# First four steps of the first block on unsplit float32 operands, in a fused attention and two-MoE kernel

## The chip, the cores and the metric

The kernel runs on one core of a Trainium2 chip. The metric is the device time of one execution in microseconds (us); lower is better. Before the change the median of three runs is 680.03 us (679.96 to 680.19). A difference of 0.2% is 1.36 us.

The engines are named as the profile names them: PE (matrix multiply) with PEld (its weight loads), DVE, ACT and POOL (elementwise work), SP (which only issues DMA loads and stores here; SPq in the trace). Each engine works through its own instructions in program order.

## The reference, cut to what matters

```python
x = window_attention(q, k, v)              # 4 x 8 heads x 576 tokens x 64, window 64
x = x.transpose(0, 2, 1, 3).reshape(2304, 512)
# first MoE layer, a plain feed-forward of 2048 hidden units:
h = x @ w_in                               # 512 -> 2048
g = where(h >= 1, h, where(h <= -1, 0, (h + 1) ** 2 / 4))
x = g @ w_out                              # 2048 -> 512
# second: 8 experts of 1024 hidden units, each token goes to one
e = argmax(x @ w_gate, axis=1)
out = gate[:, None] * (relu(x @ w1[e]) @ w2[e])
```

`w_in` and `w_out` come as 64-bit floats, everything else as 32-bit floats.

## The kernel before

**Tokens and blocks.** The 2304 tokens are 18 chunks of 128. A chunk has two attention units of four heads each (unit u = 2 x chunk + half), so there are 36 units. The first feed-forward works on five blocks of 384, 512, 512, 512 and 384 tokens (`BLOCKS`); the first block needs units 0 to 5.

**A unit** is a chain over all engines: `qk` on PE (scores, four products of 32-bit floats for each of two head pairs, line 393, after four mask products in bfloat16, line 389), `mx` on DVE (row maximum), `nm`, four exponentials `exa` to `exd` on ACT (line 427), `rb`, `rc` and `nrm` (division by the row sum, line 444, DVE or POOL), `tr` on PE (four transposes, line 471), `pb` (copy out, line 475 or 477), `av` on PE (eight products of 32-bit floats, line 486). Its result, 128 tokens by 256 values, is split into two parts that PE takes in its fast float format: `hi` (ACT, line 508) is the value rounded to that format and `lo` (DVE, line 510) is what is left.

**A feed-forward step** is one slice of 128 hidden units for one block. PE makes `h` from three passes, `w_hi x_hi`, `w_lo x_hi`, `w_hi x_lo`, of four products each (`ga`, line 603: 12 products of 384 columns in the first block). ACT and DVE make the activation (`rl`, `sq`, `st`, lines 614 to 619) and split it into `gh` and `gl` (lines 625, 627). Then `gb` (line 653) multiplies it with the same slice of `w_out`, again three passes, for three chunks: nine products of 512 columns. `acc` stays in PSUM over the sixteen steps of a block.

**A weight slice** is loaded (`lw`, 512 KB, line 292), turned from a 64-bit into a 32-bit float by one ACT and three DVE instructions (`ab`, `sa`, `sb`, `s`, lines 310 to 320) and split into two parts (`hc` on ACT, line 324; `wl` on DVE or POOL, line 326). The slices come in the order in-0, in-1, out-0, in-2, out-1, in-3, and so on; `lw`, `ab`, ... carry that place as number.

**What sets the order.** The list `HEAD` names every part of the work; each name runs one generator to its next `yield`. The order of the names is the order of the instructions on PE, DVE, ACT and POOL (`in_order`) and on SP. Tuples such as `WLO_P` or `PB_V` choose an engine for single instructions. In the first stage `lu` loads the queries and keys of a unit (320 KB, line 348), `lv` its values (256 KB, line 359). DMAs use eight semaphores in turn, so the load that is n-th on SP waits for the landing of the (n-8)-th.

PE starts with 17 products on zeros (line 1121) and a few more between the first units (`wm`, line 1241, and `KEEP_T`, line 468), which fill time in which there is no data yet. The program's later parts, which the change reaches only through the order of `HEAD` and the tuples, are the routing to experts, the second layer (lines 603 and 653 too) and the rows left over (lines 1052 to 1100).

Of the kernel before, what the change touches and what calls it, by code (L numbers as in the profile page):

```python
# [9 lines left out]
F32 = mybir.dt.float32  # L10
F32R = mybir.dt.float32r
BF16 = mybir.dt.bfloat16
I32 = mybir.dt.int32
U32 = mybir.dt.uint32
U16 = mybir.dt.uint16
ACTF = mybir.ActivationFunctionType
# [18 lines left out]
PJ_V = (3, 4, 6, 8, 11, 12, 13, 14, 19, 21, 23, 24, 26, 27, 28, 30, 35)  # L35
PS_V = ((15, 0), (17, 1))
# [4 lines left out]
ELO_P = (1, 2, 3, 7, 9, 10, 14)  # L41
LLO_P = (5, 7, 10, 13, 14)
YO_V = ((0, 3), (1, 1), (1, 2), (1, 3), (3, 0), (3, 1), (3, 2))
# [132 lines left out]
PB_V = (0, 2, 3, 6, 7, 14, 15, 16, 18, 19, 20, 23, 25, 29, 30, 31, 33, 35)  # L176
PL_V = ((15, 0), (15, 1), (31, 0), (31, 1), (47, 2), (47, 3), (63, 0), (63, 1), (63, 2), (63, 3))
PP_A = (14, 15, 16, 18, 20, 24, 25, 27, 29, 32, 33, 34)
KEEP_T = {0: 1, 1: 4}
KEEP_Q = {}  # L180
NM_P = (1, 2, 3, 7)
RB_P = (2, 5, 6, 7, 8)
# [1203 lines left out]
```

## Time and profile before

| | |
|---|---|
| median of the runs | 680.03 us |
| profiled execution | 679.67 us |
| its span, first to last instruction | 677.9 us |
| PE busy | 666.9 us (98%) |
| DVE, ACT, POOL busy | 416.1, 391.7, 105.4 us |
| granted TensorE clock, mean over the span | 0.997 |

The span is 1.77 us shorter than the profiled execution, and that is 0.36 us under the median. The chain that ended last lies on PE for 90% of the span, 43% of it in `gb` (line 653) and 42% in `ga` (line 603). In the page's slices a digit is the busy share in tenths of a slice of 16.9 us. PE is below 9 in the first and the last slice only. A matmul's record overlaps its neighbours' (they are pipelined), so what a product costs is read from the distance of starts, not from its duration.

### The profile page before, as it was taken

Reading aid. Unit: us, or ns where it says so; the run is one execution under the profiler, and the core shown is the slowest. Engines: PE = TensorE matmul, PEld = TensorE weight load, DVE = VectorE, ACT = ScalarE, POOL = GpSimd, SP = SyncE. Lnnn points to the kernel's source line nnn. Section 1 sums busy time; section 2 is a strip of 40 time slices with the busy share of each in tenths; the row PEclk is TensorE's granted clock in tenths of the full one; section 3 lists DMA queues with packets and bytes.
Section 4 is the critical chain, followed back from the end, with each engine's and each line's share of the span. In section 5 each row is a group of like instructions: output and inputs, shape, how many; then the busy total and the mean of one; then the engine's idle time right before and its main releaser. Section 6 shows DMA issues by size and latency. Waiting matters only on the chain.

```text
span 677.9 us, 11422 instructions
## 1 busy us (share of the span) xinstructions
PE 666.9 (98%) x4187; PEld 556.4 (82%) x4187; DVE 416.1 (61%) x858; ACT 391.7 (58%) x969; POOL 105.4 (16%) x93
## 2 busy tenths in 40 slices
PE   8899999999999999999999999999999999999996
PEld 4788998888888888888888889988888888888885
DVE  6999997435453414535233355889987799665541
ACT  6998887465636546545455344777666466443340
POOL 2542212300220102013101002230010000001110
PEclk9999999999999999999999999999999999999998
DMA  9993642135431313252122225344532232213342
GB/s 343 397 406 126 228 133 56 32 86 141 131 118 39 113 35 83 69 161 66 64 48 78 47 109 195 102 138 117 141 94 84 66 93 62 62 62 94 112 137 74
DMA packets 77500, 80.43 MB, mean 119 GB/s; under 512 B 46231, under 2 KB 51607, under 8 KB 77314
## 3 DMA queue, kind: packets, MB, share of 16 engines
q1 hardware_dynamic: 77138, 79.12, 37.6%
q8 instruction: 33, 0.54, 0.3%
q0 software_dynamic: 160, 0.43, 0.2%
q14 instruction: 25, 0.20, 0.1%
q10 hardware_dynamic: 144, 0.13, 0.1%
HBM read 54.32 MB, written 14.94 MB: 102 GB/s over the span
## 4 chain that ended last, share of the span: by engine, by line
PE 90%; ACT 3%; DMA 2%; DVE 1%; issue 1%; POOLq 0%; DVEq 0%; ACTq 0%; SPq 0%
PE acc L653 43%; PE h L603 42%; PE av L486 2%; PE S L393 2%; ACT sr L427 1%; DMA out_dram<-y 1%; DMA out_dram<-yl,idx 0%; DMA R<-out_dram 0%; DMA er<-in_w_dram 0%; ACT t L310 0%; PE pt L471 0%; ACT wl L842 0%; DVE wl L844 0%; DVE mx L547 0%; ACT wi L324 0%
## 5 line engine op out<-in xcount | busy, mean ns | idle before, releaser
L603 PE MATMUL h<-xT,wi 128*128 128x512 f32 (+1 forms) x960 | 208.3, 369 | 0.5 <-DVE pb L475 0.3
L603 PEld LDWEIGHTS h<-xT,wi 128*128 128x128 f32 x960 | 175.0, 188 | 25.6 <-DVE pb L475 0.6
L653 PE MATMUL acc<-wo,ghi 128*128 128x512 f32 x576 | 145.7, 393 | 0.0
L653 PEld LDWEIGHTS acc<-wo,ghi 128*128 128x128 f32 x576 | 106.9, 188 | 22.2 <-issue 0.7
L619 DVE SCALAR_TENSOR_TENSOR a<-h,a 128x512 f32<-128x512 f32 (+1 forms) x80 | 50.4, 633 | 107.9 <-ACT a L616 106.7
L614 ACT ACTIVATE a<-h,half 128x512 f32<-128x512 f32 (+1 forms) x80 | 51.6, 646 | 91.8 <-PE h L603 83.5
L603 PE MATMUL h<-xT,we 128*128 128x512 f32 (+1 forms) x480 | 103.1, 369 | 0.0
L603 PEld LDWEIGHTS h<-xT,we 128*128 128x128 f32 x480 | 84.1, 188 | 15.1
L627 POOL TENSOR_TENSOR glo<-a,ghi 128x512 fp32r<-128x512 f32 (+1 forms) x38 | 48.0, 1265 | 242.8 <-ACT ghi L625 202.2
L653 PE MATMUL acc<-wo,glo 128*128 128x512 f32 x288 | 78.4, 389 | 0.0
L653 PE MATMUL acc<-we,ghi 128*128 128x512 f32 x290 | 72.6, 389 | 0.0
L653 PEld LDWEIGHTS acc<-wo,glo 128*128 128x128 f32 x288 | 54.1, 188 | 11.5
L653 PEld LDWEIGHTS acc<-we,ghi 128*128 128x128 f32 x290 | 53.9, 188 | 10.8
L745 DVE CUSTOM_DVE_ANT_0 junk<-xg,wgb 128x512 bf16<-128x512 f32 x76 | 58.2, 766 | 2.7 <-DMA xg<-x2s 2.0
L625 ACT ACTIVATE ghi<-a 128x512 fp32r<-128x512 f32 (+1 forms) x80 | 46.5, 585 | 18.9 <-DVE a L619 11.1
L761 ACT ACTIVATE gpr<-gpr 128x512 f32<-128x512 f32 x68 | 39.8, 586 | 24.2 <-DVE gpr L753 23.5
L753 DVE TENSOR_TENSOR gpr<-xg,wgb 128x1024 f32<-128x1024 f32 x34 | 41.8, 1229 | 12.1 <-ACT gpr L761 10.4
L616 ACT ACTIVATE a<-a 128x512 f32<-128x512 f32 (+1 forms) x80 | 46.9, 588 | 1.3
L635 ACT ACTIVATE ghi<-h 128x512 fp32r<-128x512 f32 (+1 forms) x40 | 22.0, 551 | 44.0 <-PE h L603 31.1
L627 DVE TENSOR_TENSOR glo<-a,ghi 128x512 fp32r<-128x512 f32 (+1 forms) x42 | 27.7, 661 | 32.0 <-ACT ghi L625 27.7
L653 PE MATMUL acc<-we,glo 128*128 128x512 f32 (+1 forms) x145 | 39.5, 388 | 0.0
L637 DVE SCALAR_TENSOR_TENSOR glo<-h,ghi 128x512 fp32r<-128x512 f32 (+1 forms) x40 | 25.2, 633 | 20.3 <-ACT ghi L635 20.0
(176 smaller groups left out, 742.0 us busy)
## 6 DMA issues: line engine op xcount, KB each, us to landing
qk<-in_qq_dram SPq DMA_DIRECT2D x26, 320.0 KB, 4.0
er<-in_w_dram SPq DMA_DIRECT2D x32, 256.0 KB, 3.1
wraw<-in_wi_dram SPq DMA_DIRECT2D x14, 512.0 KB, 8.6
wraw<-in_wo_dram SPq DMA_DIRECT2D x14, 512.0 KB, 7.5
vt<-in_vv_dram SPq DMA_DIRECT2D x26, 256.0 KB, 3.4
xg<-x2s SPq DMA_DIRECT2D x18, 256.0 KB, 2.8
out_dram<-y SPq DMA_DIRECT2D x17, 256.0 KB, 2.3
x2s<-xrow SPq DMA_DIRECT2D x8, 512.0 KB, 3.8
```

Of the source, the lines that this page charges most:

```text
L603: nc.tensor.matmul(h[:, :n], w[:, wa, k * P:k * P + P], x[:, xa, k, o:o + n], start=(i == 0), stop=(i == 3 * KD - 1),)
L614: nc.scalar.activation(a[:, :n], h[:, :n], ACTF.Relu, scale=0.5, bias=half[:, 0:1])
L616: nc.scalar.activation(a[:, :n], a[:, :n], ACTF.Square)
L619: nc.vector.scalar_tensor_tensor(out=a[:, :n], in0=h[:, :n], scalar=1.0, in1=a[:, :n], op0=ALU.max, op1=ALU.min)
L625: nc.scalar.activation(hi[:, :n], a[:, :n], ACTF.Copy)
L627: (nc.gpsimd if pool else nc.vector).tensor_tensor(out=lo[:, :n], in0=a[:, :n], in1=hi[:, :n].bitcast(F32), op=ALU.subtract)
L635: nc.scalar.activation(hi[:, :n], h[:, :n], ACTF.Relu)
L637: nc.vector.scalar_tensor_tensor(out=lo[:, :n], in0=h[:, :n], scalar=0.0, in1=hi[:, :n].bitcast(F32), op0=ALU.max, op1=ALU.subtract,)
L653: nc.tensor.matmul(a[:, cols], ga[:, t * P:t * P + P], w[:, wa, cols], start=(first and j == 0), stop=(last and j == 2 and (not by_tile or ...
L745: nc.vector.tensor_tensor_reduce(out=junk, in0=xg[t], in1=Z["wgb"][:, e], scale=1.0, scalar=0.0, op0=ALU.mult, op1=ALU.add, accum_out=Z["L ...
L753: nc.vector.tensor_tensor(out=pr, in0=xg[t].unsqueeze(1).to_broadcast([P, 2, DM]), in1=Z["wgb"][:, e:e + 2], op=ALU.mult,)
L761: nc.scalar.activation(pr, pr, ACTF.Copy, accum_out=Z["L"][:, t, e:e + 1])
```

## The change

For the first four steps of the first block (`NF = 4`) PE multiplies the 32-bit floats themselves: one product where there were three. A weight slice of these steps can be used as soon as its 32-bit float is made (after `s`); its two parts are made later, since the other blocks use them. A unit's result in the first block is first copied whole (`xw`, a new ACT instruction), and `hi` and `lo` are made from that copy, `lo` on POOL for three of the six units (`XLO_P`). The activation of these steps isn't split: `gh` and `gl` are gone for steps 0 to 3. On PE `ga` is four products of 384 columns in these steps instead of 12, and `gb` three of 512 instead of nine. All of `HEAD` and most engine tuples are new ("order searched"); of these the diff shows a line or two.

```diff
-PB_V = (0, 2, 3, 6, 7, 14, 15, 16, 18, 19, 20, 23, 25, 29, 30, 31, 33, 35)
-KEEP_T = {0: 1, 1: 4}
+PB_V = (0, 1, 2, 3, 4, 5, 15, 17, 18, 20, 21, 24, 25, 26, 30, 31, 33)
+KEEP_T = {0: 2, 1: 5}
+NF = 4
+XLO_P = (0, 4, 5)
...
@@ -282,6 +285,7 @@
         return a.rearrange("p (a k) -> p a k", k=P)
 
     win, wout = {}, {}
+    whole_i, whole_o, whole_x = {}, {}, {}
 
     def load_w(kind, f):
         src = wi if kind == "i" else wo
@@ -305,8 +309,11 @@
 
     def split_parts(kind, f, raw):
         hw, lw = raw[:, :, 1], raw[:, :, 0]
-        t = att.tile([P, 512], I32, tag="t", name="t", bufs=TB1)
-        w = wp.tile([P, 2, 512], F32R, tag="w", name="w" + kind)
+        if f < NF:
+            t = wp.tile([P, 512], I32, tag="w", name="tw")
+        else:
+            t = att.tile([P, 512], I32, tag="t", name="t", bufs=TB1)
+            w = wp.tile([P, 2, 512], F32R, tag="w", name="w" + kind)
         nc.scalar.activation(t.bitcast(F32), hw.bitcast(F32), ACTF.Abs, scale=2.0**-112)
         yield
         nc.vector.tensor_scalar(
@@ -320,7 +327,11 @@
         nc.vector.scalar_tensor_tensor(
             out=t, in0=hw, scalar=-0x80000000, in1=t, op0=ALU.bitwise_and, op1=ALU.bitwise_or
         )
-        yield
+        if f < NF:
+            (whole_i if kind == "i" else whole_o)[f] = t.bitcast(F32)
+        yield
+        if f < NF:
+            w = wp.tile([P, 2, 512], F32R, tag="w", name="w" + kind)
         nc.scalar.activation(w[:, 0], t.bitcast(F32), ACTF.Copy)
         yield
         (nc.gpsimd if wseq_at[kind, f] in WLO_P else nc.vector).tensor_tensor(
@@ -501,10 +512,24 @@
         av = heads(bank("h" if alt else "acc", "av"))
         av_mm(s, av)
         yield
+        o = P * c - blocks[b][0]
+        if b == 0:
+            if hf not in whole_x:
+                whole_x[hf] = wp.tile([P, 2, BLOCKS[0]], F32, tag="w", name="xw")
+            xw = whole_x[hf][:, :, o:o + P]
+            nc.scalar.activation(xw, av[:, :2], ACTF.Copy)
+            del av
+            yield
         x_tile(b)
-        o = P * c - blocks[b][0]
         hi = xT[b][:, 0, 2 * hf:2 * hf + 2, o:o + P]
         lo = xT[b][:, 1, 2 * hf:2 * hf + 2, o:o + P]
+        if b == 0:
+            nc.scalar.activation(hi, xw, ACTF.Copy)
+            yield
+            (nc.gpsimd if u in XLO_P else nc.vector).tensor_tensor(
+                out=lo, in0=xw, in1=hi.bitcast(F32), op=ALU.subtract
+            )
+            return
         nc.scalar.activation(hi, av[:, :2], ACTF.Copy)
         yield
         nc.vector.tensor_tensor(out=lo, in0=av[:, :2], in1=hi.bitcast(F32), op=ALU.subtract)
@@ -606,6 +631,25 @@
                 )
                 i += 1
         return h
+
+    def whole_parts(w, n):
+
+        h = ps.tile([P, 512], F32, tag="h", name="h", bufs=2)
+        for k in range(KD):
+            nc.tensor.matmul(
+                h[:, :n], w[:, k * P:k * P + P], whole_x[k // 2][:, k % 2],
+                start=(k == 0), stop=(k == KD - 1),
+            )
+        yield
+        a = gp.tile([P, NG], F32, tag="ghi", name="aw")
+        nc.scalar.activation(a[:, :n], h[:, :n], ACTF.Relu, scale=0.5, bias=half[:, 0:1])
+        yield
+        nc.scalar.activation(a[:, :n], a[:, :n], ACTF.Square)
+        yield
+        nc.vector.scalar_tensor_tensor(
+            out=a[:, :n], in0=h[:, :n], scalar=1.0, in1=a[:, :n], op0=ALU.max, op1=ALU.min
+        )
+        return a
 
     def act_parts(x, w, o, n, pool):
         h = layer1(x, w, o, n)
@@ -1200,6 +1244,22 @@
     def step_parts(i):
         ph, b, f, t0, t1 = steps[i]
         if ph == 1:
+            if b == 0 and f < NF:
+                a = yield from whole_parts(whole_i.pop(f), blocks[0][1])
+                yield
+                for t in of_tiles(i):
+                    if began[t] == i:
+                        acc[t] = bank("acc", "acc")
+                for t in of_tiles(i):
+                    nc.tensor.matmul(
+                        acc[t], a[:, t[2] * P:t[2] * P + P], whole_o[f],
+                        start=began[t] == i, stop=ended[t] == i,
+                    )
+                del a, whole_o[f]
+                if f == NF - 1:
+                    whole_x.clear()
+                yield
+                return
             g[i] = yield from act_parts(xT[b], win[f], t0 * P, (t1 - t0) * P, i in GLO_P)
             if i == max(ended[1, b, t] for t in range(blocks[b][1] // P)):
                 del xT[b]
@@ -1251,7 +1311,7 @@
     KIND = {}
     for names, fn in (
         ("ab sa sb s hc wl", lambda k: split_parts(*pend.pop(0))),
-        ("qk mx nm exa exb exc exd rb rc nrm pp tr pb av hi lo", lambda k: (late_parts if k >= 2 * PAIR else unit_parts)(k)),
+        ("qk mx nm exa exb exc exd rb rc nrm pp tr pb av xw hi lo", lambda k: (late_parts if k >= 2 * PAIR else unit_parts)(k)),
         ("qkp mkp mxp nmp rbp rcp avp hip lop", both_parts),
         ("ga rl sq st gh gl rh rv gb", step_parts),
         ("lw", once(lambda k: pend.append(load_w(*wseq[k])))),
```

**PE, from the first step's `ga` on.** `pt` are transposes, `av` the product with the values, `h<-xT,wi` and `acc<-wo` the split steps. Before:

```order
L389 MATMUL Sa<-cb 64x128
L393 MATMUL Sa<-qqr 64x128 x4
L603 MATMUL h<-xT,wi 128x384 x12
L471 MATMUL pt<-ct,sr 128x128 x4
L603 MATMUL h<-xT,wi 128x384 x12
...
L393 MATMUL S<-qk 64x128 x4
L603 MATMUL h<-xT,wi 128x384 x12
L486 MATMUL av<-pb,vte 64x64 x8
L471 MATMUL pt<-ct,sr 128x128 x8
L603 MATMUL h<-xT,wi 128x384 x12
L486 MATMUL av<-pb,vte 64x64 x8
L653 MATMUL acc<-wo,ghi 128x512 x6
```

In the changed kernel (`h<-xw,tw` and `acc<-tw,aw` are the unsplit steps; two `ga` in a row read as x8):

```order
L404 MATMUL Sa<-qqr 64x128 x4
L639 MATMUL h<-xw,tw 128x384 x8
L482 MATMUL pt<-ct,sr 128x128 x4
L400 LDWEIGHTS cb
...
L404 MATMUL S<-qk 64x128 x4
L639 MATMUL h<-xw,tw 128x384 x4
L482 MATMUL pt<-ct,sr 128x128 x4
L497 MATMUL av<-pb,vte 64x64 x8
L482 MATMUL pt<-ct,sr 128x128 x4
L639 MATMUL h<-xw,tw 128x384 x4
L1254 MATMUL acc<-tw,aw 128x512 x3
L497 MATMUL av<-pb,vte 64x64 x16
```

The work between the first `ga` and the fourth `gb` is the same set; the first two `ga` now stand together, ahead of the transposes of unit 6, and the unit products are spread in another way.

**SP, the 22nd to 33rd load of the kernel before and the 21st to 28th of the changed one** (`qqr` and `qk` are queries and keys, `vte` and `vt` values, `wraw` weights; in brackets the semaphores that the load waits for). Before, `vte` with DMAHW6 is the values of unit 5, and `qqr` with DMAHW0 the queries of unit 9:

```order
L348 DMA qqr<-in_qq_dram 128x640 [waits DMAHW5_49]
L359 DMA vte<-in_vv_dram 128x512 [waits DMAHW6_49]
L359 DMA vte<-in_vv_dram 128x512 [waits DMAHW7_49]
L348 DMA qqr<-in_qq_dram 128x640 [waits DMAHW0_49]
L292 DMA wraw<-in_wo_dram 128x1024 [waits DMAHW1_49]
L348 DMA qk<-in_qq_dram 128x640 [waits DMAHW2_49]
L359 DMA vt<-in_vv_dram 128x512 [waits DMAHW3_49]
L359 DMA vte<-in_vv_dram 128x512 [waits DMAHW4_49]
L348 DMA qk<-in_qq_dram 128x640 [waits DMAHW5_49]
L292 DMA wraw<-in_wi_dram 128x1024 [waits DMAHW6_49]
L348 DMA qk<-in_qq_dram 128x640 [waits DMAHW7_49]
L292 DMA wraw<-in_wo_dram 128x1024 [waits DMAHW0_49,DVE_49,Activation_49]
```

Now the values of unit 5 are `vte` with DMAHW6, the queries of unit 9 the `qqr` behind it:

```order
L370 DMA vte<-in_vv_dram 128x512 [waits DMAHW4_49]
L359 DMA qqr<-in_qq_dram 128x640 [waits DMAHW5_49]
L370 DMA vte<-in_vv_dram 128x512 [waits DMAHW6_49]
L359 DMA qqr<-in_qq_dram 128x640 [waits DMAHW7_49]
L296 DMA wraw<-in_wo_dram 128x1024 [waits DMAHW0_49]
L296 DMA wraw<-in_wi_dram 128x1024 [waits DMAHW1_49]
L296 DMA wraw<-in_wo_dram 128x1024 [waits DMAHW2_49,PE_49]
L359 DMA qk<-in_qq_dram 128x640 [waits DMAHW3_49]
```

The values of unit 5 are the 23rd load in both, behind the same 22 loads in another order: `lw0` to `lw5`, `lu0` to `lu8`, `lv0` to `lv4`, the masks and the constants. The queries of unit 9 were the 25th load and are the 24th.

**ACT, shortly before the first `ga`.** Before, `xT` is `hi`, `wi` a weight's first part, `pb` the copy of a transposed unit:

```order
L508 ACTIVATE xT<-av 128x2x128
L427 ACTIVATE sr,sm<-S,nm 128x128 x2
L477 ACTIVATE pb<-pt 128x512
L310 ACTIVATE t<-wraw 128x512
L427 ACTIVATE sr,sm<-S,nm 128x128 x2
L508 ACTIVATE xT<-av 128x2x128
L477 ACTIVATE pb<-pt 128x512
L324 ACTIVATE wi<-t 128x512
L508 ACTIVATE xT<-av 128x2x128
L427 ACTIVATE sr,sm<-Sa,nm 128x128
L508 ACTIVATE xT<-av 128x2x128
L419 ACTIVATE nm<-mx 128x4
```

Now (`xw` is the whole copy, `xT<-xw` is `hi`, `tw` a weight slice on its way to a 32-bit float):

```order
L527 ACTIVATE xT<-xw 128x2x128
L438 ACTIVATE sr,sm<-S,nm 128x128 x2
L317 ACTIVATE tw<-wraw 128x512
L520 ACTIVATE xw<-av 128x2x128
L438 ACTIVATE sr,sm<-Sa,nm 128x128
L520 ACTIVATE xw<-av 128x2x128
L527 ACTIVATE xT<-xw 128x2x128
L520 ACTIVATE xw<-av 128x2x128
L438 ACTIVATE sr,sm<-Sa,nm 128x128
L527 ACTIVATE xT<-xw 128x2x128
L317 ACTIVATE tw<-wraw 128x512
L438 ACTIVATE sr,sm<-S,nm 128x128
```

The first parts of weights and the copies `pb` are gone from this stretch, and `hi` of a unit no longer stands ahead of the first `ga`: `xw` does.

## Rows read from the trace of the kernel before

**Rows 1.** The page: busy time of PE, and the slices of PE and DMA
```profile
PE 666.9 (98%) x4187; PEld 556.4 (82%) x4187; DVE 416.1 (61%) x858; ACT 391.7 (58%) x969; POOL 105.4 (16%) x93
...
PE   8899999999999999999999999999999999999996
...
DMA  9993642135431313252122225344532232213342
```

**Rows 2.** Stretches: us, each engine's busy us (count), PE clock, DMA share, GB/s
```profile
10.00:20.00 10.00, 8.80 (x177) 5.98 (x174) 9.16 (x26) 9.82 (x48) 6.76 (x9) 1.00 1.04 400
20.00:30.00 10.00, 8.53 (x159) 6.85 (x158) 9.66 (x24) 9.98 (x40) 5.01 (x8) 1.00 1.04 395
40.00:50.00 10.00, 10.00 (x78) 8.59 (x77) 10.00 (x23) 9.51 (x27) 2.05 (x2) 1.00 1.03 408
200.00:300.00 100.00, 100.00 (x630) 82.18 (x629) 36.92 (x55) 55.31 (x131) 12.04 (x9) 1.00 0.34 91
```

**Rows 3.** Timeline of PE, 26 to 62 us: start, length, instructions, idle before
```profile
27.26 2.37 PE L603 MATMUL h<-xT,wi 128*128 128x384 f32 x12
29.93 0.63 PE L471 MATMUL pt<-ct,sr 128*128 128x128 f32 x4 [0.29 <-DVE sr L444]
...
38.27 2.38 PE L603 MATMUL h<-xT,wi 128*128 128x384 f32 x12 [0.35 <-DVE pb L475]
...
51.57 0.66 PE L471 MATMUL pt<-ct,sr 128*128 128x128 f32 x4
51.98 1.64 PE L653 MATMUL acc<-wo,ghi 128*128 128x512 f32 x6
...
54.14 1.52 PE L653 MATMUL acc<-wo,ghi 128*128 128x512 f32 x6
55.50 0.84 PE L653 MATMUL acc<-wo,glo 128*128 128x512 f32 x3
56.18 2.27 PE L603 MATMUL h<-xT,wi 128*128 128x384 f32 x12
58.28 0.60 PE L471 MATMUL pt<-ct,sr 128*128 128x128 f32 x4
```

**Rows 4.** Timeline of PE, 64.1 to 64.4 us: products of 32-bit floats
```profile
64.05 0.25 PE L389 MATMUL S<-cb 64*64 64x128 bf16 x4
64.12 0.39 PE L393 MATMUL S<-qk 64*64 64x128 f32 x8
64.35 0.23 PE L389 MATMUL S<-cb 64*64 64x128 bf16 x4
```

**Rows 5.** Timeline of SP (issues), 24 to 27 us
```profile
24.16 0.33 SPq L348 DMA_DIRECT2D qk<-in_qq_dram  x1
24.84 0.33 SPq L292 DMA_DIRECT2D wraw<-in_wi_dram  x1
25.51 0.33 SPq L348 DMA_DIRECT2D qk<-in_qq_dram  x1
26.41 0.33 SPq L292 DMA_DIRECT2D wraw<-in_wo_dram  x1
```

**Rows 6.** DMA issues, 0 to 30 us: count, KB each, median us to landing
```profile
qqr<-in_qq_dram SPq DMA_DIRECT2D x10, 320.0 KB, 7.0
...
vte<-in_vv_dram SPq DMA_DIRECT2D x9, 256.0 KB, 7.0
```

**Rows 7.** Waits of PE, 0 to 60 us: total us, times, longest
```profile
PE av L486 <- DMA vte<-in_vv_dram: 0.5, 1, 0.5
```

**Rows 8.** Chain of waits, 20 to 30 us: start, us, what
```profile
25.22 0.49 ACT pb L477
25.71 0.52 ACT wi L324
26.23 0.27 ACT xT L508
```

More of the change, by code (lines that the diff above doesn't have):

```diff
@@ L34 @@
 EARLY = 10
-PJ_V = (3, 4, 6, 8, 11, 12, 13, 14, 19, 21, 23, 24, 26, 27, 28, 30, 35)
-PS_V = ((15, 0), (17, 1))
+PJ_V = (1, 2, 4, 5, 6, 8, 9, 15, 17, 19, 21, 24, 25, 26, 27, 30, 31, 34)
+PS_V = ((15, 0), (15, 1), (16, 1), (17, 0), (17, 1))
 DT0 = 14
@@ L40 @@
 PBB = 2
-ELO_P = (1, 2, 3, 7, 9, 10, 14)
-LLO_P = (5, 7, 10, 13, 14)
-YO_V = ((0, 3), (1, 1), (1, 2), (1, 3), (3, 0), (3, 1), (3, 2))
+ELO_P = (0, 5, 8, 10, 13, 15)
+LLO_P = (2, 3, 4, 7, 8, 9, 12, 13, 14, 15)
+YO_V = ((2, 0), (3, 2), (3, 3))
 SCRATCH = 4096
@@ L58 @@
 HEAD = (
[112 rows of a table removed]
-).split()
-NRM_P = (0, 1, 2, 3, 4, 5, 8, 9, 10, 14, 15, 16, 17, 20, 21, 28, 30, 31, 33, 34)
-WLO_P = (2, 3, 4, 6, 20, 22, 27, 28)
-GLO_P = (0, 3, 4, 5, 6, 9, 15, 18, 19, 20, 21, 24, 26, 27, 29, 30, 31, 34, 36, 37, 39, 40, 41, 46, 48, 50, 51, 52, 54, 56, 59, 67, 68, 69, 70, 72, 73, 77)
-PB_V = (0, 2, 3, 6, 7, 14, 15, 16, 18, 19, 20, 23, 25, 29, 30, 31, 33, 35)
-PL_V = ((15, 0), (15, 1), (31, 0), (31, 1), (47, 2), (47, 3), (63, 0), (63, 1), (63, 2), (63, 3))
-PP_A = (14, 15, 16, 18, 20, 24, 25, 27, 29, 32, 33, 34)
-KEEP_T = {0: 1, 1: 4}
[113 rows of a table added]
+).split()
+NRM_P = (0, 1, 2, 3, 4, 5, 7, 8, 9, 12, 15, 16, 17, 19, 27, 28, 30, 33, 34, 35)
+WLO_P = (1, 3, 6, 13, 16, 20, 26, 28, 30)
+GLO_P = (13, 18, 19, 21, 23, 25, 34, 35, 37, 39, 41, 43, 45, 49, 51, 54, 56, 57, 59, 62, 64, 65, 66, 67, 69, 70, 72, 79)
+PB_V = (0, 1, 2, 3, 4, 5, 15, 17, 18, 20, 21, 24, 25, 26, 30, 31, 33)
+PL_V = ((15, 0), (15, 1), (15, 2), (31, 3), (63, 0), (63, 2), (63, 3))
+PP_A = (15, 16, 24, 25, 30, 32, 35)
+KEEP_T = {0: 2, 1: 5}
 KEEP_Q = {}
-NM_P = (1, 2, 3, 7)
-RB_P = (2, 5, 6, 7, 8)
+NM_P = (0, 1, 6, 7, 8)
+RB_P = (3, 4, 6, 7, 8)
+NF = 4
+XLO_P = (0, 4, 5)
 WARM = 17
```

225 rows, old and new, of the table HEAD are left out of this document.

## The prediction

> **What bounds the kernel now.** I read the page first: PE is busy for 98% of the span, and its slices are full except the first and the last [rows 1]. So the time is PE's work, plus what PE loses at both ends. The table of stretches then says where it loses: from 10 to 30 us PE is busy for 8.5 to 8.8 of every 10 us, from 40 us on for all of it [rows 2]. In the first 30 us two other things are full as well: ACT, with 9.82 and 9.98 of 10 us, and the DMA engines, with a share of 1.04 at 395 to 400 GB/s [rows 2]. At 200 to 300 us ACT is at 55 of 100 and DMA at 0.34, with PE at 100 [rows 2]. What the change does is thus worth what it does to one moment: the one from which PE never waits again. PE's timeline shows it. The first `ga` starts at 27.26, behind it there are two waits that the profile names, 0.29 and 0.35 us, and from 38.27 on there is none [rows 3]. I take the start of the seventh `ga`, 56.18 us [rows 3], as the mark: the same work stands before it in both kernels, and behind it PE runs full. What moves the mark moves the end.
>
> **What the change takes from PE and adds to it.** In an undisturbed place a split `ga` (12 products of 384 columns) takes 2.10 us, from 56.18 to 58.28, and a split `gb` (nine of 512) 2.04 us, from 54.14 to 56.18 [rows 3]. The fifth step and all later ones stay split.
>
> No row shows a product of 32-bit floats over the whole array, so its price is bounded by the nearest rows. The scores are such products, on quarters of the array. The order lists four of them where the trace counts eight instructions: a product is two instructions. Eight of 128 columns take from 64.12 to 64.35, and as four quarters work side by side that is two in a row, 0.115 us each, 0.90 ns per column [rows 4]. A transpose is one such instruction over the whole array: four of 128 columns from 51.57 to 51.98 are 0.80 ns per column [rows 3]. So an unsplit `ga` is 4 x 2 x 384 columns, 2.46 to 2.76 us, and an unsplit `gb` is 3 x 2 x 512 columns, also 2.46 to 2.76 us. Against 2.10 and 2.04 a step grows by 0.36 + 0.42 = 0.78 to 0.66 + 0.72 = 1.38 us, four steps by 3.1 to 5.5 us. I take the middle, 4.3, since a dense product has the scores' form and the transposes' place in the array. All of it is on PE, the bound, and nothing hides it; only an earlier start can pay for it.
>
> A rule of the Trainium skill bears on this (FP8 and Floating Point Precision, TensorE Precision Notes): a true FP32 product takes four passes through the array. By that, with a pass at the price that a pass has here (2.10 / 12 = 0.175 us for 384 columns, 2.04 / 9 = 0.227 for 512 [rows 3]), `ga` would be 16 passes, 2.80 us, and `gb` 12 passes, 2.72 us; four steps would grow by 5.5 us. The rows' own rate gives 3.1 to 5.5, so the rule stands at the dear end.
>
> **What the earlier start gives back.** Before the first `ga`, ACT no longer makes first parts of weights (0.52 us each) nor copies of transposed units (0.49), and the whole copy takes the place of `hi` (0.27) [rows 8]; DVE loses the second parts and the `lo`. If those queues alone decided, the first `ga` would come about 2 us earlier: two weight parts and three copies are 1.04 + 1.47 = 2.5 us, less about two early `hi`, 0.5. But the loads don't move. Each load waits for the landing of the eighth before it, so issues are landings: the 31st issue, at 24.84, tells of the 23rd landing [rows 5], and PE did wait 0.5 us for values once [rows 7]. The 23rd load is the values of unit 5 in both kernels, with the same 22 loads ahead. The queries of unit 9 are now the 24th. Before, the 24th (256 KB) landed at 25.51, 0.67 us later [rows 5, 6]; 320 KB take 0.84, so they land at 25.68. On PE the scores of unit 9 still stand ahead of the first `ga`; two head pairs at 0.30 us (64.05 to 64.35 [rows 4]) end at 26.28. So the first `ga` starts at about 26.3 and not at 27.26: 1.0 us gained, and hardly more than 1.5 even if the scores of unit 9 cost nothing, because values that land at 24.84 have still to go through PE and ACT.
>
> **The waits behind it.** The first one (0.29, on the division of unit 6) goes, because two `ga` now stand ahead of that transpose; the second (0.35, on a copy `pb`) should go too, since the longer products give ACT and DVE more time. That is 0.64 us [rows 3]. Between none and about 1.1 us is possible, since some starts behind them are late as well.
>
> **What costs nothing.** The deferred parts of eight weight slices, six copies `xw` and the missing `gh` and `gl` of four steps all lie on ACT, DVE and POOL. They are needed for the second block at the earliest, and PE has over 60 us of queued work by then; ACT and DVE have room from 100 us on (at 200 to 300 us 55 and 37 of 100 [rows 2]). If that cover failed, each late part would cost one ACT instruction, 0.5 us. The two more fillers ahead of transposes stand in time that PE waits anyway. The new order behind the first block can't gain where PE has no gap [rows 1, 2]; it can lose, and I allow nothing for it.
>
> **The sum.** -1.0 for the start, +4.3 for the products, -0.64 for the waits: +2.7 us. The profiled execution is 679.67 us, so 682.3; the median of the runs lies 0.36 us above it, so 682.7. With the bounds (products 3.1 to 5.5, start -1.5 to -0.5, waits -1.1 to 0) the likeliest case has 681.0 to 685.0, and mostly 681.4 to 684.3.
>
> **Rivals.**
>
> 1. *No change that can be told.* The loads are not the limit, because a reordered queue lands its first pieces sooner, and the first `ga` starts 2 us earlier; products at the cheap end. -2.0 + 3.1 - 0.64 = +0.5, or 680.5. For it: ACT was just as full as the DMAs. Against it: the 22 loads ahead are the same.
> 2. *Faster.* An instruction of a dense 32-bit product streams its columns once, at the pass price: `ga` 8 x 0.175 = 1.40, `gb` 6 x 0.227 = 1.36, so each step shrinks by 1.38 us, four by 5.5; with the start and the waits -7.1. ACT, full until 40 us, would give PE perhaps half of it: 673 to 676.5. The point from which the sign turns: the 6144 columns of a step's instructions may cost 4.14 + 0.41 us (0.41 is a quarter of the 1.64 gained), 0.74 ns per column. Both rows lie above it, 0.80 and 0.90, so I give it little. A line of the Trainium skill may be read that way (Perfetto Trace Analysis, Engine Utilization: half the output rate for FP32_LOW_HIGH); read for one product it gives this rival, read for each of the two instructions it gives the rows.
> 3. *Slower by more.* The activation of an unsplit step lies in the three buffers that `ghi` has. The fourth step's first ACT instruction must wait until the first `gb` has read the first buffer, and ACT's queue stands behind it: parts of weights 4 and 5 and the copies of units. The first `gb` comes late, about 40 us, and ends 2.6 us later; ACT would stand for 2 us. From the point on where the fifth `ga` waits for its weight this reaches PE: +2, 684.7.
> 4. *The order elsewhere.* The last slice has PE at 6 tenths [rows 1]; a better order of the end could win 2 us, 680.7 with the rest of the sum, or more than the sum.
>
> **Chances.** Likeliest case 0.56, rival 1 0.21, rival 2 0.08, rival 3 0.10, rival 4 0.05. About 0.2%, 1.36 us, is what a measurement can tell from no change. Slower by more than that: most of the likeliest case and rival 3, 0.63. Within it: rival 1, the rest of the likeliest and some of rival 4, 0.25. Faster: rival 2 and the rest of rival 4, 0.12. The range 679.0 to 684.8 leaves out rival 2 and the far end of rival 3.
>
> **What will show it.** In the new trace: starts of unsplit `ga` 2.5 to 2.8 us apart and unsplit `gb` likewise (rival 2: 1.4); the first `ga` at 26.3, with the scores of unit 9 just ahead (rival 1: by 25.3); the seventh `ga` at 58.8 and not 56.18; no wait of PE behind it. I am wrong if the first `ga` starts before 25 us, or if the seventh stands by 57 us, or if the two kernels differ by more than 1 us between that mark and the end.

## The result, and the profile after

The changed kernel takes 683.82 us (median of 5 runs, 683.75 to 684.92), the kernel before 680.03 (679.73 to 681.26): 3.79 us slower, ratio 1.0056 with a 95% interval of 1.0042 to 1.0071. The profiled execution took 684.03 us with a span of 682.3, at a granted clock of 0.997 as before. The forecast was 682.7, so the sign and the range held and the sum was 1.1 us short. The two profiled executions lie 4.36 us apart and not 3.79, because before's is 0.36 us under its median and the changed kernel's 0.21 over.

The page of the changed kernel, PE's busy time and instructions [rows 1]:

```profile
PE 671.8 (98%) x4161; PEld 551.5 (81%) x4161; DVE 414.6 (61%) x857; ACT 391.8 (57%) x969; POOL 101.2 (15%) x92
```

PE has 26 instructions less (16 in `ga`, 12 in `gb`, and two fillers more) and is busy for 4.9 us more. The extra time is PE work, not waiting. A stretch at the start (columns as in [rows 2]):

```profile
20.00:30.00 10.00, 9.76 (x174) 6.99 (x167) 9.61 (x21) 9.46 (x41) 4.53 (x8) 1.00 1.04 398
```

From 20 to 30 us PE is busy for 9.76 us where it was 8.53, and ACT got room: 9.46 where it was 9.98. The timeline of PE (start, length, instructions, idle before), to be laid beside [rows 3]:

```profile
26.76 5.43 PE L639 MATMUL h<-xw,tw 128*128 128x384 f32 x16
32.02 0.60 PE L482 MATMUL pt<-ct,sr 128*128 128x128 f32 x4
...
33.78 2.85 PE L639 MATMUL h<-xw,tw 128*128 128x384 f32 x8
36.47 0.60 PE L482 MATMUL pt<-ct,sr 128*128 128x128 f32 x4
...
38.20 2.82 PE L639 MATMUL h<-xw,tw 128*128 128x384 f32 x8
40.86 2.74 PE L1254 MATMUL acc<-tw,aw 128*128 128x512 f32 x6
43.53 1.15 PE L497 MATMUL av<-pb,vte 128*64 128x64 f32 x32
...
57.86 4.73 PE L628 MATMUL h<-xT,wi 128*128 128x384 f32 x24
62.52 0.25 PE L400 MATMUL S<-cb 64*64 64x128 bf16 x4
```

Two unsplit `ga` in a row take 32.02 - 26.76 = 5.26 us, 2.63 each; the others 36.47 - 33.78 = 2.69 and 40.86 - 38.20 = 2.66; an unsplit `gb` 43.53 - 40.86 = 2.67. No wait stands between the first `ga` and the mark. The mark's record begins at 57.86 while the `gb` ahead still runs; two undisturbed split `ga` (2 x 2.10, [rows 3]) end at 62.52, so the mark lies at 58.3, 2.1 us later than before.

PE's waits show one that is new (waiter, releaser: us in total, times, longest), to be laid beside [rows 7]:

```profile
PE h L628 <- DVE a L663: 0.5, 1, 0.5
```

It stands at 114 us, far behind the mark. (The one for values `vte` that before had with 0.5 us is there with 0.9.) All engines just ahead of it:

```profile
109.31 1.20 DVE L566 TENSOR_TENSOR S<-S,cb 128x1024 f32<-128x1024 f32 x1
...
110.42 1.54 DVE L327 SCALAR_TENSOR_TENSOR t<-sraw,t 128x512 int32<-128x512 int32 x1
...
112.00 0.63 ACT L335 ACTIVATE wo<-t 128x512 fp32r<-128x512 f32 x1 [2.29 <-DVE t L327]
...
114.00 1.20 PE L628 MATMUL h<-xT,wi 128*128 128x512 f32 x4 [0.50 <-DVE a L663]
```

ACT stands for 2.29 us in front of one weight part (`hc30`, line 335), because DVE makes its input (line 327) behind a mask sum of 1.20 us. The steps of an activation (lines 660 and 663) queue behind it, and PE waits for the activation.

The end of the program, first before, then after: SP's loads of the rows `R`, PE's last product, and DVE's last sums, which need `R`.

```profile
668.60 0.82 SPq L906 DMA_DIRECT2D R<-out_dram  x2
...
671.15 0.28 PE L653 MATMUL acc<-we,glo 128*128 128x256 f32 x1
671.40 0.75 DVE L874 SCALAR_TENSOR_TENSOR y<-acc,gm,R 128x512 f32<-128x512 f32 x1 [3.22 <-DMA R<-out_dram]
```

```profile
672.25 0.82 SPq L950 DMA_DIRECT2D R<-out_dram  x2
...
674.84 0.28 PE L697 MATMUL acc<-we,glo 128*128 128x256 f32 x1
675.77 0.75 DVE L918 SCALAR_TENSOR_TENSOR y<-acc,gm,R 128x512 f32<-128x512 f32 x1 [2.55 <-DMA R<-out_dram]
```

PE's last product starts at 674.84; before it was 671.15. So the 2.1 us at the mark became 3.7 at the last product, and the last sum is 4.4 us later. It waits for a load `R` in both kernels: the two loads are issued about as long before the last product (2.55 and 2.59 us), but the sum follows the first issue by 2.80 us before and by 3.52 now. The difference of 4.4 is therefore 2.1 ahead of the mark, 1.6 between mark and last product, 0.7 behind it.

How exact is one trace? Up to the mark three more kernels below have the start of the changed one. The first `ga` of e4, then of e6 (in e9 it is at 26.77):

```profile
28.03 5.43 PE L636 MATMUL h<-xw,tw 128*128 128x384 f32 x16
```

```profile
26.18 5.43 PE L636 MATMUL h<-xw,tw 128*128 128x384 f32 x16
```

So the same start lies between 26.18 and 28.03 us, and the mark moves along with it. The five traces with the start of before (before, e7, e8, e10, e11) have 27.26 to 27.51. What is said of the start from one trace is no finer than that; times between two places behind the first `ga` repeat better: from it to the record of the mark the four kernels need 30.9 to 31.1 us.

### The profile page after: what moved, and what is told of

It reads as the page before. It is cut to its first block, busy times and chain, and to the rows that moved or that the text cites. A ratio compares the mean times of both kernels' runs of the same rounds, so it can differ in the third digit from the quotient of the medians.

```text
span 682.3 us, 11376 instructions
## 1 busy us (share of the span) xinstructions
PE 671.8 (98%) x4161; PEld 551.5 (81%) x4161; DVE 414.6 (61%) x857; ACT 391.8 (57%) x969; POOL 101.2 (15%) x92
## 4 chain that ended last, share of the span: by engine, by line
PE 82%; DVE 7%; DMA 5%; ACT 4%; issue 1%; SPq 1%; DVEq 0%; ACTq 0%
PE acc L697 39%; PE h L628 38%; PE av L497 2%; PE S L404 1%; DVE t L327 1%; DVE t L323 1%; DMA wraw<-in_wo_dram 1%; DMA qqr<-in_qq_dram 1%; DMA vte<-in_vv_dram 1%; DMA wraw<-in_wi_dram 1%; PE accl L1136 1%; PE hl L1108 1%; DVE t L319 1%; ACT sr L543 1%; DVE wi L337 1%
## 5 line engine op out<-in xcount | busy, mean ns | idle before, releaser
L628 PE MATMUL h<-xT,wi 128*128 128x512 f32 (+1 forms) x912 | 199.9, 372 | 0.5 <-DVE a L663 0.5
L628 PEld LDWEIGHTS h<-xT,wi 128*128 128x128 f32 x912 | 166.6, 188 | 26.7 <-issue 1.3
L697 PE MATMUL acc<-wo,ghi 128*128 128x512 f32 x552 | 139.2, 392 | 0.0
L697 PEld LDWEIGHTS acc<-wo,ghi 128*128 128x128 f32 x552 | 102.7, 188 | 21.0 <-issue 0.3
L658 ACT ACTIVATE a<-h,half 128x512 f32<-128x512 f32 (+1 forms) x76 | 49.0, 647 | 91.5 <-PE h L628 81.9
L697 PE MATMUL acc<-wo,glo 128*128 128x512 f32 x276 | 75.1, 390 | 0.0
L671 POOL TENSOR_TENSOR glo<-a,ghi 128x512 fp32r<-128x512 f32 (+1 forms) x28 | 35.1, 1254 | 237.2 <-ACT ghi L669 196.8
L789 DVE CUSTOM_DVE_ANT_0 junk<-xg,wgb 128x512 bf16<-128x512 f32 x76 | 55.1, 725 | 5.0 <-DMA xg<-x2s 2.9
L671 DVE TENSOR_TENSOR glo<-a,ghi 128x512 fp32r<-128x512 f32 (+1 forms) x48 | 31.5, 660 | 26.0 <-ACT ghi L669 20.5
L660 ACT ACTIVATE a<-a 128x512 f32<-128x512 f32 (+1 forms) x76 | 44.2, 590 | 1.0
```

What stands on the lines that cost most here:

```text
L628: nc.tensor.matmul(h[:, :n], w[:, wa, k * P:k * P + P], x[:, xa, k, o:o + n], start=(i == 0), stop=(i == 3 * KD - 1),)
L658: nc.scalar.activation(a[:, :n], h[:, :n], ACTF.Relu, scale=0.5, bias=half[:, 0:1])
L660: nc.scalar.activation(a[:, :n], a[:, :n], ACTF.Square)
L671: (nc.gpsimd if pool else nc.vector).tensor_tensor(out=lo[:, :n], in0=a[:, :n], in1=hi[:, :n].bitcast(F32), op=ALU.subtract)
L697: nc.tensor.matmul(a[:, cols], ga[:, t * P:t * P + P], w[:, wa, cols], start=(first and j == 0), stop=(last and j == 2 and (not by_tile or ...
L789: nc.vector.tensor_tensor_reduce(out=junk, in0=xg[t], in1=Z["wgb"][:, e], scale=1.0, scalar=0.0, op0=ALU.mult, op1=ALU.add, accum_out=Z["L ...
```

## Experiments

All kernels were timed beside the kernel before on the same chip. The table gives each median less that of before beside it. That median of before is 680.03 us in the first row and 680.51 to 680.76 in the others, so two rows have to differ by more than half a microsecond to be told apart.

| kernel | median, us | above before, us | ratio, 95% interval |
|---|---|---|---|
| changed kernel | 683.82 | 3.79 | 1.0042 to 1.0071 |
| e1_f32_old_order | 684.77 | 4.01 | 1.0050 to 1.0078 |
| e2_split_new_order | 696.34 | 15.58 | 1.0217 to 1.0245 |
| e3_loads | 685.31 | 4.55 | 1.0057 to 1.0085 |
| e4_hc30 | 683.84 | 3.08 | 1.0028 to 1.0056 |
| e5_eight_steps | 693.9 | 13.39 | 1.0163 to 1.0202 |
| e6_tail | 687.28 | 6.77 | 1.0087 to 1.0116 |
| e7_zeros_together | 695.58 | 15.07 | 1.0207 to 1.0239 |
| e8_zeros_apart | 695.79 | 15.28 | 1.0212 to 1.0245 |
| e9_tail_late | 683.33 | 2.62 | 1.0022 to 1.0047 |
| e10_half_together | 700.2 | 19.49 | 1.0270 to 1.0301 |
| e11_half_apart | 717.23 | 36.52 | 1.0525 to 1.0557 |
| e12_start | 683.4 | 2.69 | 1.0024 to 1.0052 |

### Is it the products or the order?

**e1_f32_old_order**: four unsplit steps, in the order and with the engine choices of before. In `HEAD` each early `hi` becomes the whole copy, `hi` and `lo` come later, `gh` and `gl` of four steps go; the parts of the weights stay as early as they were:

```diff
-... hi0 ... hi1 ... lo1 ... lo0 ... hi2 ...
+... xw0 ... xw1 ... xw2 ... (hi0 lo0 hi1 lo1 ... behind the first products)
-gh0 gl0 gh1 gl1 gh2 gl2 gh3 gl3
```

> The unsplit first four steps alone, in the order and with the engine choices of the kernel before; hi and lo of the first block are made behind the first products. Theory A (the products cost 4.7 us on PE, and the order is a smaller matter): first ga near 27.0, +4.7 for the products, 1 to 2 us back from waits and handovers behind the first ga, so 682.3 to 683.4 us. Rival B (the new order is what costs): 680.7 us or less.

It is as slow as the changed kernel. Its PE timeline:

```profile
39.53 2.85 PE L636 MATMUL h<-xw,tw 128*128 128x384 f32 x8 [0.77 <-DVE pb L483]
42.31 0.69 PE L494 MATMUL av<-pb,vte 128*64 128x64 f32 x16
42.92 5.42 PE L1251 MATMUL acc<-tw,aw 128*128 128x512 f32 x12
48.18 0.60 PE L479 MATMUL pt<-ct,sr 128*128 128x128 f32 x4
...
62.38 0.60 PE L479 MATMUL pt<-ct,sr 128*128 128x128 f32 x4
...
675.29 0.28 PE L694 MATMUL acc<-we,glo 128*128 128x256 f32 x1
```

Two unsplit `gb` take 5.26 us. The `ga` at the mark ends at 62.38 and not at 58.28 [rows 3], 4.1 us later, and the last product is 4.1 us later, too. So the unsplit products cost about 4 us by themselves (0.4 of the 4.1 is a grown wait), and with the order of before behind it a late mark costs nothing more. The time lies above the range of the theory: 4.01 us over before, where the theory's 682.3 to 683.4 lie 2.3 to 3.4 over the 680.03 of the result. One of the two waits that I expected to go has grown instead (0.77 for a copy `pb`, 0.35 before [rows 3]).

**e2_split_new_order**: the new order with split steps; parts, `gh` and `gl` put back into `HEAD` by hand:

```diff
-NF = 4
+NF = 0
+hc1 wl1 hc0 wl0 ... gh0 gl0 ... gh3 gl3    (each behind what it needs)
```

> The order of the changed kernel with split operands in all steps: parts of the first weights and of the first block's units put back near where their inputs are made, not tuned. Theory A: 4.7 us less on PE, 1 to 2.5 us given back by a later first ga, so 680.0 to 681.6 us. Rival B: 683 us or more, since the order stays.

The time is far above both numbers. It satisfies rival B's "683 us or more", but not for B's reason, as the waits of PE show:

```profile
PE h L625 <- ACT pb L485: 3.7, 2, 2.1
PE pt L479 <- POOL sr L452: 3.2, 3, 1.4
```

Before, the longest that PE waits for these is 0.35 us [rows 3]. I take it that the parts that I put back stand in queues that have no room for them there; no other placing was tried. The run says nothing on the price of a product, and so decides nothing between the two.

**e5_eight_steps**: e1 with eight unsplit steps; the parts of eight more weight slices are made behind their products.

```diff
-NF = 4
+NF = 8
```

> The kernel of e1_f32_old_order (order of before) with eight unsplit steps instead of four; the parts of the weights of steps 4 to 7 are made behind their products. Theory A (every unsplit step costs PE 0.55 us in ga and 0.63 us in gb, less 0.1 to 0.3 us of handovers that go): e5 stands 3.5 to 4.5 us above e1's distance to before, that is 7.5 to 8.5 us above before. Rival (what e1 lost is a single loss at the start, in the order): e5 is within 1 us of e1, 3 to 5 us above before.

It goes up, as products that cost something in every step demand and a single loss at the start doesn't. The size is no clean dose: 9.4 us above e1 is over twice what I expected. Some 4 us of it stand in one place, at 472 us, where PE waits for 2.1 us and the granted clock falls after that. Stretches (columns as in [rows 2]) and two waits:

```profile
475.00:476.00 1.00, 1.00 (x5) 0.81 (x4) 1.00 (x4) 0.00 (x0) 0.00 (x0) 0.67 0.00 0
476.00:477.00 1.00, 1.00 (x4) 0.71 (x4) 1.00 (x2) 0.00 (x0) 0.00 (x0) 0.50 0.00 0
478.00:479.00 1.00, 1.00 (x5) 0.76 (x4) 0.74 (x3) 0.98 (x4) 0.00 (x0) 0.62 0.00 0
```

```profile
PE h L625 <- DVE a L660: 2.1, 1, 2.1
...
PE pt L479 <- DVE sr L546: 0.8, 1, 0.8
```

Without these 4 us, 5.4 are left for four more steps. The second wait, at 93 us, is new as well, and without it 4.6 are left, 1.1 a step, where e1 has 1.0. Why PE comes to wait there, and not in e1, wasn't tried.

### What sets the start?

**e3_loads**: the loads of two weight slices moved behind the queries of unit 9, with the operations on them.

```diff
-lw4 lw5 ... lu9
+lu9 lw4 lw5    (ab4 sa4 sb4 ab5 sa5 later, too)
```

> The changed kernel with the weight loads lw4 and lw5 (1 MB) moved behind the queries of unit 9, and their first ACT and DVE instructions with them. Theory A (the loads set the start of the first ga): the first ga starts at 24.5 to 25.3 us and not at 26.8, time 681.6 to 682.5 us. Rival C (ACT and DVE set it): the first ga stays within 0.4 us, 683.5 to 684 us.

The first `ga` did not come sooner than in the changed kernel (26.76), though the queries of unit 9 landed 3.2 us sooner, so these loads alone don't set it. An issue tells of the landing of the eighth load before it: the 32nd issue of the changed kernel and the 30th of e3 tell of these queries. SP in the changed kernel, then SP and PE in e3, then PE's waits in e3:

```profile
26.12 0.33 SPq L296 DMA_DIRECT2D wraw<-in_wi_dram  x1
```

```profile
22.95 1.05 SPq L367 DMA_DIRECT2D vt<-in_vv_dram  x1
...
26.89 1.56 PE L636 MATMUL h<-xw,tw 128*128 128x384 f32 x4
```

```profile
PE pt L479 <- POOL sr L546: 0.7, 1, 0.7
PE pt L479 <- DVE aw L646: 0.6, 1, 0.6
PE S L397 <- DMA cb<-in_msk_dram: 0.6, 1, 0.6
PE pt L479 <- POOL sr L452: 0.6, 2, 0.3
```

The first scores wait 0.6 us for the masks here (0.4 in the changed kernel), and transposes 0.6 us for POOL's divisions (line 452), for which the changed kernel's waits have no such line, and from 23.4 us to the first `ga` PE has work without a named wait. The two waits of the first lines come behind the first `ga`. The kernel stands 0.8 us further above before than the changed one, but the intervals overlap.

**e12_start**: e9 (below) with the chain of unit 5 ahead of other work on DVE and PE, and the first `ga` ahead of the scores of unit 9.

```diff
-tr5 ab5 av4 qk8 mx7 xw4 nm7 pb5 av5 ... xw3 ... xw5 ... qk9 ... ga0
+tr5 pb5 ab5 av4 xw4 xw3 xw5 av5 qk8 ga0 mx7 ... qk9
```

(A name runs the next part of its unit, so `xw5 av5` are `av` and then `xw`.)

> e9_tail_late with another order just ahead of the first ga: the copy pb of unit 5 ahead of a row maximum on DVE, av and xw of unit 5 ahead of the scores of unit 8 on PE, and the first ga ahead of the scores of unit 9. Theory J (values of unit 5 land at 24.8, then av and xw, 0.6 and 0.4 us): first ga at 25.8 to 26.0 and not 26.76, and 0.3 to 0.9 us less than e9. Rival K (ACT and DVE are full and set the start in any order): first ga at 26.5 or later, time as e9 or above.

PE's timeline in e12:

```profile
24.89 0.69 PE L494 MATMUL av<-pb,vte 128*64 128x64 f32 x16 [0.60 <-DMA vte<-in_vv_dram]
...
26.18 2.85 PE L636 MATMUL h<-xw,tw 128*128 128x384 f32 x8
...
58.04 4.21 PE L625 MATMUL h<-xT,wi 128*128 128x384 f32 x21
```

The values of unit 5 are there at 24.89, and the first `ga` moved from 26.77 to 26.18, 0.2 to 0.4 us less than expected. Still the mark is not earlier (58.04 as recorded, 57.87 in e9), since from the first `ga` to there e12 needs 31.9 us and e9 31.1; and the time is that of e9. PE now waits 0.60 us for the values, in a place where it did the scores of unit 8 in e9. The first `ga` came sooner only because other PE work was put behind it. A start is no gain where PE's idle time ahead of it stays.

### What is lost behind the mark?

**e4_hc30**: the changed kernel with the one weight part of 112 us behind the activation.

```diff
-... hc30 ... st16 ...
+... st16 hc30 ...
```

> The changed kernel with one ACT instruction, the first part of weight slice 30, moved behind the activation of step 16 that stood behind it. Theory A: PE's wait of 0.5 us at 113 us goes and the time falls by 0.5 to 0.7 us, to 683.2 us. Rival D (PE has slack there that is used up later): no change, 683.8 us.

The median is 683.84 us, which is rival D's number, and that of the changed kernel 683.82; only the distance to before beside it falls, by 0.7 us, and the intervals overlap. So the times decide nothing, but the traces do, since PE has the same instructions in the same order in both. The seventh `ga` and the last product in e4:

```profile
58.95 4.73 PE L625 MATMUL h<-xT,wi 128*128 128x384 f32 x24
...
674.95 0.28 PE L694 MATMUL acc<-we,glo 128*128 128x256 f32 x1
```

In this execution e4 is 1.1 us behind the changed kernel at the mark (57.86 there), ahead of anything that was changed, and only 0.1 us at the last product (674.84). 0.8 of the 1.0 us are won at the moved part: over the same products, with the wait between them, PE needs 112.67 to 116.86 us in the changed kernel and 113.61 to 117.00 in e4, where the wait for the activation is gone. That is a little more than was expected.

**e6_tail**: the changed kernel up to the seventh `ga`, then the order and the engine choices of before.

```diff
 HEAD = (order of the changed kernel up to ga6)
-       (its order behind it)
+       (the order of before, less what is done)
```

> The changed kernel up to the seventh ga, and from there on the order and the engine choices of before. Theory D (what the two kernels differ by behind the mark, 2.3 us, is the searched order, not the later mark): the mark stays at 57.9, and the time is 1.7 to 2.4 us above before, about 682.3. Rival E (a later mark makes later work collide in any order): 3.5 us or more above before, as in the changed kernel.

Inconclusive: the two orders don't fit together there. At that moment they have done different parts of the weights, and the join brings a wait of its own (at 94 us):

```profile
PE pt L479 <- ACT pb L485: 2.1, 1, 2.1
```

**e9_tail_late**: the same with the join at the sixteenth `ga`, about 112 us, where both have done nearly the same set of work (edit as in e6, `ga15` for `ga6`).

> The changed kernel up to the sixteenth ga (about 112 us, where both kernels have done nearly the same set of work), and from there on the order and engine choices of before. Theory D (the searched order behind the first block costs 1.4 us behind 110 us and 0.7 us after the last product): 1.4 to 2.4 us less than the changed kernel's distance to before, that is 1.4 to 2.4 us above before. Rival E (a later mark makes later work collide in any order): 3.5 us or more above before.

It stands 2.62 us above before, 1.2 us less than the changed kernel and a little less of a gain than I expected at least; by the intervals, which overlap, the two could be equal. Its trace: PE's last product, then DVE's last sum.

```profile
673.80 0.28 PE L694 MATMUL acc<-we,glo 128*128 128x256 f32 x1
```

```profile
674.02 0.75 DVE L915 SCALAR_TENSOR_TENSOR y<-acc,gm,R 128x512 f32<-128x512 f32 x1 [3.20 <-DMA R<-out_dram]
```

Its mark is that of the changed kernel (2.1 us after before's), its last product comes 2.65 us after before's and not 3.7, and the last sum 2.6 and not 4.4. (The whole spans, 681.5 and 682.3, differ by 0.8 only: from its last sum to its end e9 takes a microsecond longer, and that wasn't traced.) Together with e1 and e4 this says that the searched order, not the late mark, cost most of what was lost there. With e12 it is the fastest of the kernels with unsplit steps, and none beats the kernel before.

### What lies around a 32-bit product?

**e7_zeros_together** and **e8_zeros_apart**: before, with four products of 32-bit zeros added onto the sum inside each of the 16 `ga` of the third block. In e7 all four stand behind the sixth fast product, in e8 singly.

```diff
+                for _ in range(z.count(i)):
+                    nc.tensor.matmul(h[:, :P]..., ident, zf..., start=False, stop=False)
-            g[i] = yield from act_parts(..., i in GLO_P)
+            g[i] = yield from act_parts(..., i in GLO_P, (6, 6, 6, 6) if b == 2 else ())   # e8: (3, 5, 7, 9)
```

> Before, with four products of 32-bit floats (128 columns, zeros, added onto the sum) inside each of the 16 ga of the third block, all four behind the sixth fast product. Their own price by the rows of before, 64 x 2 x 128 columns at 0.80 to 0.90 ns, is 13.1 to 14.7 us. Theory F (a handover between fast and 32-bit products costs PE 0.11 to 0.17 us): 32 handovers more, so 16.6 to 20.1 us above before. Rival G (a handover is free; what PE lost around 32-bit products were waits): 13.1 to 14.7 us.

> The same 64 products, but each by itself: behind the 3rd, 5th, 7th and 9th fast product of each of the 16 ga. 128 handovers instead of 32. Theory F: 96 x 0.11 to 0.17 = 10.6 to 16.3 us above e7. Rival G: within 1 us of e7.

e8 is 0.2 us above e7, with 96 handovers between formats more: a handover between fast and 32-bit products over the whole array costs nothing that could be measured, and my theory of a price for it falls. e7 lies 15.07 us above before, 0.235 us for each of 64 products: 0.4 above the own price that I worked out, which is rival G's range, and 1.5 below what the theory asked.

**e10_half_together** and **e11_half_apart**: the same two with weights of 64 columns, so that the zero products use half the array, as `av` does.

```diff
-nc.tensor.matmul(h[:, :P]..., ident, zf..., start=False, stop=False)
+nc.tensor.matmul(h[:64, :P]..., ident[:, :64], zf..., start=False, stop=False)
```

> e7_zeros_together, but each zero product uses half of the array's columns (weights of 64 columns, as in av). 32 changes between the full and the half array. Theory H (a change of the array's shape costs PE 0.10 to 0.15 us, as the rows around av in both traces have it): 32 x 0.10 to 0.15 = 3.2 to 4.8 us above e7, or somewhat less if the smaller weights load sooner. Rival I (shape is free, as the handover between formats was): within 1 us of e7 or below it.

> e8_zeros_apart with half-array zero products: 128 changes of shape. Theory H: 96 x 0.10 to 0.15 = 9.6 to 14.4 us above e10. Rival I: within 1 us of e10, as e8 stood to e7.

Now the same 96 changes cost 17.0 us, 0.18 us each, a little more than the theory had. The 32 of e10 cost 4.4 us (19.49 - 15.07), 0.14 each; that comparison is less clean, as the weights have half the size. PE's timelines, e8 and then e11:

```profile
252.60 0.38 PE L611 MATMUL h<-zf,ct 128*128 128x128 f32 x2
...
253.29 0.38 PE L611 MATMUL h<-zf,ct 128*128 128x128 f32 x2
```

```profile
252.57 0.43 PE L611 MATMUL h<-zf,ct 128*64 128x128 f32 x2
...
253.60 0.43 PE L611 MATMUL h<-zf,ct 128*64 128x128 f32 x2
```

The fourth column tells them apart: 128*128 in the one, 128*64 in the other. From one zero product to the next it is 0.69 us in e8 and 1.03 in e11, with two fast products between them and, in e11, two changes of shape. The Trainium skill says that changing the tiling mode drains the TensorE (TensorEngine Tiling (Array Packing), Key Properties). A cost at every change agrees with that, and the runs give the price, 0.14 to 0.18 us a change between these two shapes.

## Why the prediction was right, and where not

1. **The bound.** Right: PE's own work decides. It is busy for 4.9 us more, with fewer instructions.
2. **The products, "4.3".** The mechanism held: 2.63 to 2.69 us for an unsplit `ga` and 2.67 for a `gb`, within the bounds of 2.46 to 2.76. (The Trainium skill's four passes, FP8 and Floating Point Precision, TensorE Precision Notes, made 2.80 and 2.72 in the prediction's estimate; the rows lie a little under that.) The size was off on the other side of the subtraction. I took a split `ga` at 2.10 us, from an undisturbed place. The four that were replaced stood among transposes, scores and `av`; one of them, with the `av` behind it:

```profile
33.91 2.38 PE L603 MATMUL h<-xT,wi 128*128 128x384 f32 x12
36.22 0.69 PE L486 MATMUL av<-pb,vte 128*64 128x64 f32 x16
```

   It takes 2.31 us, and so does the one at 38.27 [rows 3]. In their places the change is 2.65 - 2.32 for a `ga` (means of four, named waits taken off) and 2.66 - 2.10 for a `gb`, 0.89 us a step and 3.6 in all. In e1, which keeps the order of before, an unsplit `ga` ahead of an `av` takes 2.78 (42.31 - 39.53), so the unsplit product grows there, too. Part of it is the array's shape: from the first `ga` to the mark it changes ten times before and eight times now, 0.3 to 0.4 us at the price of e10 and e11. The rest of what a place costs wasn't traced.
3. **The start, "-1.0".** It was -0.5: 26.76 and not 26.3. The chain that was worked out is there, later by the landings: the 32nd issue, which tells of the queries of unit 9, stands at 26.12 and not at 25.68, and the first `ga` follows by 0.64, where 0.60 was forecast. The step that failed is "the loads decide": in e3 these queries land 3.2 us sooner and the first `ga` is at 26.89, since PE's own queue, with its small waits for masks, values and divisions, ends at the same moment as the loads. e12 shows that an earlier `ga` doesn't bring the mark forward either. And the difference of 0.5 is smaller than the scatter of the same start over four traces.
4. **The waits, "-0.64".** Both named waits are gone. From the first `ga` to the mark before needs 56.18 - 27.26 = 28.9 us and the changed kernel 58.3 - 26.76 = 31.5, 2.6 more. The products and the waits make 3.6 - 0.64 = 3.0 of it. The missing 0.4 us is the fifth and the sixth `ga`, which are split in both kernels: before, each stands ahead of an `av` and takes 2.28 and 2.29 us (45.77 to 48.05, 48.66 to 50.95). Now each follows a `gb`, and the pair takes 4.77 us (44.61 to 49.38, 49.81 to 54.58), 2.10 more than the 2.67 of a `gb`. With the start the mark is at +2.1 and not +2.7.
5. **"Nothing" behind the mark.** Wrong, and by the prediction's own condition: the kernels differ by 2.3 us between the mark and the end, more than the 1 us that was allowed. The cause is rival 4's, with the other sign: the order elsewhere lost time. e1 shows that the order of before loses nothing there. Of the 1.6 us ahead of the last product one weight part at 112 us makes 0.8 (e4), and e9, whose order replaces that place, wins 1.0; where the rest is lost stays open. The 0.7 us at the load `R` has a reason in the list: it calls the two loads as `xr1 ... xr0`, before as `xr0 ... xr1`, and the first sum needs that of `xr0`, now the second. e9, with the order of before at its end, is back at 2.80 us from the first issue (671.22) to the sum. A run that swaps these two alone wasn't made.
6. **Rival 3**, the buffer of the activation: no such wait is in the trace. **Rival 1**, the start 2 us earlier: not so. **Rival 2**, columns streamed once: the rows have 2.63 us and not 1.40.

So the errors at the mark (0.6 us too much) and behind it (2.3 too little) partly offset each other in the profiled execution; the forecast's sum is better than its parts, and that is luck. (The low end of the likeliest case is 680.5 by its own bounds, not 681.0; nothing hangs on it.)

## What to carry to other kernels

Take the price of what is removed from the place where it stands, not from the cleanest place of the trace: around other shapes of product the same 12 instructions took 2.3 us and not 2.1. Where PE is full, judge a start by the PE work and idle time ahead of a later mark; an early first product that only swaps places with other work is worth nothing. And a list that sets all of the order is a change everywhere: even where no instruction is added, look for the one queue in which something needed stands behind something that isn't. Last, compare traces place by place: the same start moved by almost 2 us from one execution to another, while e4, with the same instructions on PE, showed a gain of 0.8 us at the place that was changed, which its median did not show.

## What was not expected of the hardware

- A change of the array's shape between 128*128 and 128*64 costs PE 0.14 to 0.18 us (e10, e11); a handover between fast and 32-bit products of one shape costs nothing that could be measured (0.2 us for 96, e8).
- A small 32-bit product (128 columns, own weights) takes 0.235 us for its two instructions, 0.92 ns a column; in long ones (384 columns) it is 2.63 / (8 x 384), 0.86 ns.
- In e5 PE stood still for 2.1 us until 473.8 us. Up to 475 us the granted clock was at its full level (2.4 GHz); in the stretches from 476 to 478 us, with PE busy again, it was at 0.50 (1.2 GHz), and at 1.00 again from 479, with 0.67 and 0.62 in the stretches between. By these four stretches the lower level cost about 1.7 us beside the wait.
